# Folding the biases early, q one step ahead, the mask read from SBUF, and narrower scores for the first tile, in a fused attention and mixture-of-experts kernel

## The chip, the cores and the metric

The kernel runs on one core of a Trainium2 chip. The metric is device microseconds of one execution, as the median of several executions; lower is better. The compared kernel before the change took 1164.09 us.

## The reference

Attention over 4 batches, 8 heads, 768 positions and 64 dimensions, and behind it a mixture of 4 experts on the 3072 rows that the attention gives:

```python
scores = (1 / sqrt(64)) * (q @ k.T)                       # per batch and head
rel = pos[:, None] - pos[None, :]
is_global, is_local = pos[None, :] < 8, (rel >= 0) & (rel < 96)
dist = where(is_global & ~is_local, 96, abs(rel))
scores = where(is_global | is_local, scores - slope[h] * dist, -1e9)
x = softmax(scores) @ v                                   # then heads side by side: 3072 x 512
p = domain_probs / (domain_probs.sum(-1) + 1e-9)
out = sum over e of p[:, e] * (relu(x @ w1[e]) @ w2[e])   # w1: 512 x 1024, w2: 1024 x 512
```

A query attends to at most 95 positions before its own and 8 global ones, so a tile of 128 queries needs the keys of its own 128 positions, of the 96 before, and the global ones.

## The kernel before, in words

**Stages.** The program runs in three stretches. First the attention of batch 0 (`attention_early`), alone on the chip, to about 62 us. Then the expert layers of batches 0 and 1, unit by unit, and between their products the attention of batches 1, 3 and 2 (`attention_chain`), which ends within the first 664 us. The rest, to the end, is the expert layers of batches 2 and 3 (`late_batch`); the change does not touch it.

**The expert layers.** They are written with sums of blocks (the scheme of Strassen and Winograd), so that seven products stand for eight. A unit's `first(i)` makes the seven products `pm<-xT,w1s` and `pm<-xB,w1s`, each of six matmuls 384 columns wide; VectorE (DVE) adds such a product to others (`u`, `vv`, `pm`) and, with ScalarE (ACT), leaves `h`. `second(i)` multiplies `h` by w2 (`pm<-w2s,h`, 36 matmuls 512 wide). The weights come by DMA as `raw` and are cast or summed into `w1s` and `w2s` by ACT and GpSimd (POOL). The products have four PSUM buffers of their own.

**The attention of batches 1, 3 and 2.** The work goes by pairs of heads, 12 of them (`order`, lines 626 to 698), and a pair by six tiles t of 128 queries. A tile goes through a pipeline of four stages, one stage at each call of `flow`: `scores` (line 410), `softmax` in two calls (440), `turn_folded` (512), and, when six tiles have gathered, `weigh` (528).

- `prepare_q` and `prepare_k` turn a half of q or k (three tiles) by `pt<-ident,q` or `pt<-ident,k` on TensorE (PE). The value is kept as a rounded part and its remainder, each in the type fp32r: ACT writes the rounded part (`qd<-pt`, `kd<-pt`), DVE the remainder. For q, `spread_q` then copies both parts to the other 64 partitions by DMA from ACT's queue (`qd<-qd`), and the scores wait for that.
- `scores` makes, for each of two heads, two matmuls `ps<-kd,qd`: stationary are 128 columns of q, moving are 256 columns of k's window. So a tile has four. The first tile (t = 0) has no earlier keys, but is 256 wide too.
- `softmax` adds the bias `nbias` (DVE, which also takes the extreme `nmax`), takes the exponential (ACT, `pb`), and one call later scales by the reciprocal of the sum into `pn` (ACT). In `pn` the columns lie folded: global columns share a block with others.
- `turn_folded` transposes `pn` on PE into a PSUM bank `pt`. ACT copies it to SBUF (`pT`), and DVE makes from the same PSUM tile the masked part of the earlier keys with the triangle `newer` (one `scalar_tensor_tensor`).
- `weigh` multiplies `pT` by v (`pt<-pT,v`) and by differences of v (`pt<-pT,vg`), three tiles into one PSUM bank, twice. ACT copies each half to `x`.

The pool `pt` has two PSUM banks. Transposes of q, k and `pn` and the two halves of `weigh` all go through them, and a bank is free again when its last reader is done.

**The order of the work.** A step of the chain (up to a `yield`) is put between the steps of the expert layers by a count: 149 steps before (`count`, line 1425), spread evenly. In the first two stretches and the last one the engines keep the program's order. In the middle one, from about the chain's first step, a scheduler of the language sets the order on each engine from its own estimates, so that an edit in one place can move instructions elsewhere. Instructions of all engines but the DMA issues on SP go through one helper (`emit`, line 42), which is why the profile's lines all name L43.

**The folding.** The table `nbias` (8 heads, 352 columns, bf16) is laid out for the first attention. The other one wants it otherwise, so the chain's first step (line 656) makes the triangle `newer` on POOL, takes a minimum over 96 columns of each head and copies four pieces on DVE.

**A pair's steps, before:** q's first half, k's first half with the spreading of q, q's second half; then t = 0; k's second half, t = 1; the loads of the next pair's q and k, t = 2; the differences of v, t = 3; t = 4; t = 5. These are twelve. v of the pair is loaded at its t = 0.

## Time and profile before

| | |
|---|---|
| three runs | 1163.98, 1164.09, 1166.28 us; median 1164.09 |
| the profiled execution | 1165.77 us, of which 1164.0 us are the span of the profile |
| granted TensorE clock | 0.997 of full speed over the span |
| PE busy | 1137.0 us, 98% |
| DVE, ACT, POOL busy | 882.2, 630.8, 625.8 us (76, 54, 54%) |

Busy time is the time in which an engine had an instruction under way. The order of reading: which engine is busy nearly all of the time, then what its idle time waits for (the releaser, behind the arrow), and what of the other engines' time lies beside it. A group of instructions in a row is named by its tiles, written before the arrow, read behind it, with partitions x elements.

### The profile page before, as it was taken

The numbers are of one execution on the slowest core, as the hardware profiler recorded it, in microseconds if no ns is written. First come the engines' busy times: TensorE is split into PE (matmuls) and PEld (weight loads), VectorE is DVE, ScalarE is ACT, GpSimd is POOL, SyncE is SP. The second block draws the span as 40 slices with busy tenths as digits, with TensorE's granted clock in tenths as the row PEclk, the third lists the DMA queues.
The fourth block names the chain that finished last, engine by engine and source line by source line (L and its number), as shares of the span: only waits on it lengthen the run. The fifth ranks groups of instructions, "written<-read, shape, count | busy, mean of one in ns | idle before, by whom it ended". The sixth has DMA issues, their size and how long they took to land.

```text
span 1164.0 us, 21323 instructions
## 1 busy us (share of the span) xinstructions
PE 1137.0 (98%) x7414; PEld 1056.0 (91%) x7414; DVE 882.2 (76%) x2069; ACT 630.8 (54%) x1777; POOL 625.8 (54%) x606
## 2 busy tenths in 40 slices
PE   7899999999999999999999999999999999999997
PEld 5678898988898989889898899999999999999997
DVE  7978778777878777787777777777777777777776
ACT  6844777877753665665675334444444444444443
POOL 5667656555453234322222427777778855555554
PEclk9999999999999999999999999999999999999999
DMA  9547989787776888987968668888887687676763
GB/s 183 150 141 277 300 216 305 246 258 198 288 245 227 277 264 264 272 245 241 278 187 277 212 217 301 307 301 301 287 314 280 244 296 249 241 258 227 258 228 132
DMA packets 180978, 290.80 MB, mean 250 GB/s; under 512 B 86784, under 2 KB 137472, under 8 KB 168576
## 3 DMA queue, kind: packets, MB, share of 16 engines
q1 hardware_dynamic: 172992, 273.63, 71.6%
q10 hardware_dynamic: 7872, 15.74, 4.7%
q8 instruction: 61, 1.00, 0.4%
q14 instruction: 53, 0.43, 0.1%
HBM read 207.93 MB, written 70.78 MB: 239 GB/s over the span
## 4 chain that ended last, share of the span: by engine, by line
PE 86%; POOL 4%; DVE 4%; DMA 2%; ACT 2%; issue 2%; ACTq 0%; POOLq 0%; DVEq 0%
PE pm L43 36%; PE pf L43 19%; PE X L43 11%; PE Y L43 9%; PE pt L43 7%; PE ps L43 3%; POOL w1s L43 1%; DMA qd<-qd 1%; DVE pb L43 1%; POOL sums L43 1%; PE px L43 1%; POOL xT L43 1%; POOL xB L43 1%; POOL w2s L43 1%; DMA raw<-in_moe_w_dram 1%
## 5 line engine op out<-in xcount | busy, mean ns | idle before, releaser
L43 PE MATMUL pm<-w2s,h 128*128 128x512 f32 x1152 | 284.6, 396 | 2.6 <-DVE h L43 1.6
L43 PEld LDWEIGHTS pm<-w2s,h 128*128 128x128 f32 x1152 | 210.6, 188 | 45.9 <-DVE h L43 3.8
L43 ACT ACTIVATE hf<-pf 128x384 f32<-128x384 f32 x128 | 62.8, 492 | 248.3 <-DVE pf L43 247.1
L43 POOL TENSOR_TENSOR hS<-sf,hS 128x384 fp32r<-128x384 f32 x126 | 134.2, 1084 | 112.4 <-ACT hS L43 111.6
L43 DVE SCALAR_TENSOR_TENSOR acc<-pm,prob,acc 128x512 f32<-128x512 f32 x180 | 132.6, 747 | 34.1 <-PE pm L43 31.7
L43 PE MATMUL pm<-xT,w1s 128*128 128x384 f32 x744 | 148.7, 341 | 0.0
L43 PE MATMUL pf<-xT,w1s 128*128 128x384 f32 x768 | 146.5, 335 | 0.9 <-ACT hf L43 0.7
L43 POOL TENSOR_TENSOR sums<-raw 128x256 f32<-128x256 f32 x54 | 38.8, 737 | 183.3 <-DMA raw<-in_moe_w_dram 91.2
L43 PEld LDWEIGHTS pf<-xT,w1s 128*128 128x128 f32 x768 | 131.4, 188 | 1.7 <-ACT hf L43 1.2
L43 PEld LDWEIGHTS pm<-xT,w1s 128*128 128x128 f32 x744 | 127.7, 188 | 0.8 <-issue 0.7
L43 DVE TENSOR_TENSOR hA<-hf,hA 128x384 fp32r<-128x384 f32 x94 | 84.6, 926 | 50.6 <-ACT hA L43 50.6
L43 PE MATMUL pm<-xB,w1s 128*128 128x384 f32 x574 | 118.4, 345 | 2.5 <-DVE h L43 2.4
L43 ACT ACTIVATE pb<-pb,nmax 128x160 f32<-128x160 f32 (+2 forms) x192 | 84.4, 447 | 48.9 <-DVE nmax L43 44.6
L43 PE MATMUL pf<-xB,w1s 128*128 128x384 f32 x576 | 110.7, 335 | 0.2 <-ACT hf L43 0.2
L43 PEld LDWEIGHTS pm<-xB,w1s 128*128 128x128 f32 x574 | 99.4, 188 | 8.2 <-DVE h L43 2.8
L43 ACT ACTIVATE h<-pm 128x384 fp32r<-128x384 f32 x128 | 62.2, 491 | 70.0 <-DVE pm L43 66.5
L43 PEld LDWEIGHTS pf<-xB,w1s 128*128 128x128 f32 x576 | 98.7, 188 | 0.5 <-ACT hf L43 0.4
L43 POOL TENSOR_TENSOR sf<-hf 128x384 f32<-128x384 f32 x63 | 70.4, 1117 | 43.6 <-ACT hf L43 43.6
L43 ACT COPY pT<-pt 128x256 f32<-128x256 f32 (+2 forms) x216 | 71.1, 329 | 21.7 <-DVE pT L43 12.7
L43 DVE SCALAR_TENSOR_TENSOR h<-pm,h 128x384 fp32r<-128x384 f32 x128 | 69.6, 551 | 10.6 <-ACT h L43 9.1
L43 PE MATMUL Y<-w2b,hS 128*128 128x256 f32 x576 | 74.0, 282 | 0.0
L43 PE MATMUL X<-w2b,hS 128*128 128x256 f32 x576 | 73.9, 282 | 0.0
(168 smaller groups left out, 2250.7 us busy)
## 6 DMA issues: line engine op xcount, KB each, us to landing
w1s<-kept SPq DMA_DIRECT2D x47, 1792.0 KB, 8.0
w2b<-kept SPq DMA_DIRECT2D x224, 256.0 KB, 4.2
kept<-w1s SPq DMA_DIRECT2D x16, 1792.0 KB, 7.7
raw<-in_moe_w_dram SPq DMA_DIRECT2D x43, 512.0 KB, 5.2
kept<-w2s SPq DMA_DIRECT2D x16, 1024.0 KB, 9.2
w2s<-kept SPq DMA_DIRECT2D x16, 1024.0 KB, 6.2
qd<-qd ACTq DMA_DIRECT2D x48, 192.0 KB, 4.3
q<-in_q_dram SPq DMA_DIRECT2D x30, 192.0 KB, 5.1
```

The lines of the kernel that those rows point to most:

```text
L43: ins = fn(*args, **kwargs)
```

## The change

Four edits, all in the attention.

1. **The fold.** It moves into a function `fold_biases`, called at the 27th step of the first attention, before that attention ends. The minimum stays on DVE; the copies, now three, are POOL's. The layout of the first tile's columns changes with it.
2. **q ahead.** The first half of the next pair's q is prepared at the step of t = 4 and spread there. So a pair has 11 steps: k's first half, q's second half; t = 0; k's second half, t = 1; (the load of this pair's v) t = 2; t = 3; the next q's first half, t = 4; t = 5. The loads of the next pair's q and k move to t = 1 and t = 3, the differences of v to t = 4. `count` becomes 138.
3. **The mask.** In `turn_folded` DVE reads ACT's copy `pT` in place of the PSUM tile `pt`.
4. **The first tile.** Its scores are 128 columns wide instead of 256 (four matmuls in each of 12 pairs), and its `pn` is written in four pieces of 96 and 32 columns by ACT, in place of two of 128.

The diff:

```diff
--- before.py
+++ after.py
@@ -410,12 +410,12 @@
     def scores(A, t, got):
 
         both = A.ps.tile([P, 2, 2 * P], F32, name="ps")
-        c0 = (NQT - 1 - t) * PL - (0 if t else NPREV)
+        c0, n = ((NQT - 1 - t) * PL, 2 * P) if t else ((NQT - 1) * PL - NGLOB, P)
         for j in range(2):
-            win = got["k"][:, j].rearrange("p t c -> p (t c)")[:, c0 : c0 + 2 * P]
+            win = got["k"][:, j].rearrange("p t c -> p (t c)")[:, c0 : c0 + n]
             for part in range(2):
                 te.matmul(
-                    both[:, j],
+                    both[:, j, :n],
                     got[("q", t // TPH)][:, j, part, t % TPH * P : (t % TPH + 1) * P],
                     win,
                     start=(part == 0),
@@ -450,8 +450,8 @@
                 new["pcol"] = pcol = slice(P, width) if t == 0 else slice(0, width)
             else:
                 width = PL
-                cols = slice(NPREV, NPREV + P) if t == 0 else slice(0, width)
-                bcol = slice(PL, PL + P) if t == 0 else slice(0, width)
+                cols = slice(0, P) if t == 0 else slice(0, width)
+                bcol = slice(2 * P, 3 * P) if t == 0 else slice(0, width)
                 new["pcol"] = pcol = slice(0, P) if t == 0 else slice(0, width)
                 if t:
                     both = new["both"]
@@ -491,10 +491,16 @@
 
             old["pn"] = pn = A.pb.tile([P, 2 * PL], F32, name="pn")
             if old["t"]:
-                pieces = ((0, pn[:, :PL], pb[:, 0]), (1, pn[:, PL : PL + NGLOB], pb[:, 1, P:]))
+                pieces = (
+                    (0, pn[:, :PL], pb[:, 0]), (1, pn[:, PL : PL + NGLOB], pb[:, 1, P:]),
+                    (1, pn[:, PL + NGLOB :], pb[:, 1, :P]),
+                )
             else:
-                pieces = ((0, pn[:, :P], pb[:, 0, :P]),)
-            for j, dst, src in (*pieces, (1, pn[:, PL + NGLOB :], pb[:, 1, :P])):
+                pieces = [
+                    (j, pn[:, j * (PL + NGLOB) + to : j * (PL + NGLOB) + to + n], pb[:, j, fro : fro + n])
+                    for j in range(2) for to, fro, n in ((0, NGLOB, NPREV), (NPREV, 0, NGLOB))
+                ]
+            for j, dst, src in pieces:
                 ac.activation(dst, src, AF.Copy, scale=zsum[:, j : j + 1])
 
     def turn(A, tile_):
@@ -517,13 +523,14 @@
         for place, at in enumerate((0, PL + NGLOB, P)[: 3 if t else 2]):
             te.transpose(pt[:, place, :], pn[:, at : at + P], ident)
         if t:
-            ve.scalar_tensor_tensor(
-                pT[:NPREV, 0], newer[:NPREV, None, :P].to_broadcast([NPREV, 2, P]), 1.0, pt[:NPREV, :2],
-                op0=ALU.subtract, op1=ALU.mult,
-            )
             for j in range(2):
                 ac.copy(pT[NPREV:, 0, j], pt[j * NGLOB : (j + 1) * NGLOB, 2])
         ac.copy(pT[:, 1], pt[:, :2])
+        if t:
+            ve.scalar_tensor_tensor(
+                pT[:NPREV, 0], newer[:NPREV, None, :P].to_broadcast([NPREV, 2, P]), 1.0, pT[:NPREV, 1],
+                op0=ALU.subtract, op1=ALU.mult,
+            )
 
     def weigh(A, three, x, b):
 
@@ -623,6 +630,16 @@
             flow()
             yield
 
+    def fold_biases():
+
+        po.iota(
+            newer, pattern=[[1, P + NGLOB]], base=1 - NGLOB, channel_multiplier=-1, allow_small_or_imprecise_dtypes=True
+        )
+        po.tensor_scalar(newer, newer, 0.0, 1.0, op0=ALU.is_gt, op1=ALU.mult)
+        ve.tensor_tensor(nbias[:, :, :NPREV], nbias[:, :, :NPREV], nbias[:, :, PL : 2 * P], op=ALU.min)
+        for to, fro in ((PL, NPREV), (NPREV, P), (P, PL)):
+            po.tensor_copy(nbias[:, :, to : to + NGLOB], nbias[:, :, fro : fro + NGLOB])
+
     def attention_chain(bs, A):
 
         tiles, turned = [None] * 4, []
@@ -654,43 +671,42 @@
                     nats[m][n] = next(load(A, {"q": q, "k": k, "v": v}[n], *order[m], n))
 
         fetch_heads(0, "qkv")
-        po.iota(
-            newer, pattern=[[1, P + NGLOB]], base=1 - NGLOB, channel_multiplier=-1, allow_small_or_imprecise_dtypes=True
-        )
-        po.tensor_scalar(newer, newer, 0.0, 1.0, op0=ALU.is_gt, op1=ALU.mult)
-        ve.tensor_tensor(nbias[:, :, :NPREV], nbias[:, :, :NPREV], nbias[:, :, PL : 2 * P], op=ALU.min)
-        for to, fro, n in (
-            (PL, 2 * P + NGLOB, NPREV), (2 * P + NGLOB, NPREV, NGLOB), (NPREV, P, NGLOB), (P, 2 * P + NGLOB, NGLOB),
-        ):
-            ve.tensor_copy(nbias[:, :, to : to + n], nbias[:, :, fro : fro + n])
-        yield
+        yield
+        prepare_q(A, nats[0]["q"], 0, gots[0])
+        flow()
+        yield
+        spread_q(0, gots[0])
         for m, (b, pr) in enumerate(order):
             if pr == PAIRS[0]:
                 xs[b] = None if b == B - 1 else xp.tile([P, NPAIR, S], F32, name="x")
                 if b == B - 1:
                     xd[b] = dp.tile([P, NPAIR, S], F32, name="x_last")
             nat, got = nats[m], gots[m]
-            for part, hf in ((prepare_q, 0), (prepare_k, 0), (prepare_q, 1)):
+            for part, hf in ((prepare_k, 0), (prepare_q, 1)):
                 part(A, nat[part.__name__[-1]], hf, got)
                 flow()
-                if part is prepare_k:
-                    spread_q(0, got)
                 yield
             for t in range(NQT):
-                if t in (1, 2, 3):
-                    if t == 1:
-                        prepare_k(A, nat["k"], 1, got)
-                    elif t == 2:
-                        fetch_heads(m + 1, "qk")
-                    else:
-                        nat["vg"] = differences(A, nat["v"])
+                if t == 1:
+                    prepare_k(A, nat["k"], 1, got)
+                if t == 4 and m + 1 < len(order):
+                    prepare_q(A, nats[m + 1]["q"], 0, gots[m + 1])
+                if t in (1, 2, 4):
                     flow()
+                    if t == 2 and m:
+                        fetch_heads(m, "v")
                     yield
                 flow({"t": t, "pr": pr, "m": m, "v": nat})
                 if t == 0:
                     spread_q(1, got)
-                if t == 0 and m:
-                    fetch_heads(m, "v")
+                elif t == 1:
+                    fetch_heads(m + 1, "q")
+                elif t == 3:
+                    fetch_heads(m + 1, "k")
+                elif t == 4:
+                    if m + 1 < len(order):
+                        spread_q(0, gots[m + 1])
+                    nat["vg"] = differences(A, nat["v"])
                 yield
         while any(tiles):
             flow()
@@ -1047,6 +1063,8 @@
             work_chores()
             if n == 4 * NQT + 1:
                 opening(A)
+            if n == 4 * NQT + 2:
+                fold_biases()
         mix = mixture()
         next(mix)
     Ordered.on = False
@@ -1422,7 +1440,7 @@
 
     SUMUNITS = tuple(per + i for i in (0, 1, 3, 4, 5, 7, 8, 9, 11, 12, 13))
     todo_t = [units[i][1:] for i in range(per)]
-    count, span = 3 * NPAIR * (6 + NQT) + 5, (LATE * 13 * per - 12) * 0.97
+    count, span = 3 * NPAIR * (5 + NQT) + 6, (LATE * 13 * per - 12) * 0.97
     emitted = done = paced = 0
     Ordered.on = True
     for _ in first_sums(1):
```

Where the scheduler moves instructions, three places. The first is PE at the weighing of the second pair of heads (`pT,v` and `pT,vg` are `weigh`'s products, `w2s,h` those of `second`, `w1s` those of `first`). Before:

```order
L43 MATMUL pt<-pT,v 64x128 x4
L43 MATMUL pt<-pT,vg 64x128 x2
L43 MATMUL pt<-pT,v 64x128 x2
L43 MATMUL pt<-pT,vg 64x128 x2
L43 MATMUL pt<-pT,v 64x128 x2
L43 MATMUL pt<-pT,vg 64x128 x2
L43 MATMUL pt<-pT,v 64x128 x2
```

With the change:

```order
L43 MATMUL pt<-ident,k 128x128 x3
L43 MATMUL pt<-pT,v 64x128 x4
L43 MATMUL pt<-pT,vg 64x128 x2
L43 MATMUL pt<-pT,v 64x128 x2
L43 MATMUL pt<-pT,vg 64x128 x2
L43 MATMUL pm<-w2s,h 128x512 x4
L43 MATMUL pt<-pT,v 64x128 x2
L43 MATMUL pt<-pT,vg 64x128 x2
L43 MATMUL pt<-pT,v 64x128 x2
```

Before, the weighing was one run, the two halves in the two `pt` banks. Now four products of `second` stand between the halves, and both halves use one bank. (An F32 product such as `pT,v` shows in the trace as two records.) In 11 of the 12 pairs the halves are apart now, by four or five products.

The second place is ACT around its copy `x<-pt` of the same weighing. Before:

```order
L43 ACTIVATE h<-pm 128x384
L43 DMA qd<-qd 64x768
L43 ACTIVATE h<-pm 128x384
L43 DMA qd<-qd 64x768
L43 ACTIVATE h<-pm 128x384
L43 COPY x<-pt 128x384 x2
L43 ACTIVATE pb,zsum<-pb,nmax 128x128 x2
L43 CAST w1s<-raw_2652 128x512
```

With the change:

```order
L43 ACTIVATE h<-pm 128x384
L43 ACTIVATE pb,zsum<-pb,nmax 128x128
L43 CAST kd<-pt 64x3x128 x2
L43 ACTIVATE zsum<-zsum 128x2
L43 CAST w1s<-raw_2652 128x512
L43 COPY x<-pt 128x384
L43 CAST w1s<-raw_2652 128x256
L43 CAST w1s<-sums 128x512
```

The first copy stood behind nothing of the weights; now it stands behind the casts of k (`kd<-pt`) and a cast of w1 (`w1s<-raw`), which waits for a DMA. Five of the pairs have the cast of w1 there.

The third place is the fold, on DVE. Before, between the sums of `first`'s products:

```order
L43 TENSOR_TENSOR u<-pm,p_1187 128x384
L43 TENSOR_TENSOR nbias<-nbias 128x8x96
L43 TENSOR_TENSOR vv<-pm,u 128x384
L43 COPY nbias<-nbias 128x8x96
L43 COPY nbias<-nbias 128x8x32
L43 TENSOR_TENSOR u<-pm,u 128x384
L43 COPY nbias<-nbias 128x8x32
L43 TENSOR_TENSOR pm<-pm,vv 128x384
L43 COPY nbias<-nbias 128x8x32
L43 TENSOR_TENSOR pm<-pm,p_1187 128x384
```

With the change, between the first attention's last softmax and the first operands of the expert layers:

```order
L43 TENSOR_SCALAR pb,spare<-pb,zsum 128x256 x2
L43 TENSOR_SCALAR zsum,spare<-zsum 128x2
L43 RECIPROCAL zsum<-zsum 128x2
L43 TENSOR_SCALAR pb,spare<-pb,zsum 128x256 x2
L43 TENSOR_TENSOR nbias<-nbias 128x8x96
L43 TENSOR_TENSOR xB_736<-x 128x384
L43 TENSOR_TENSOR xB_735<-xB_736,x 128x384
L43 TENSOR_TENSOR xB_735<-x,xB_735 128x384
```

The minimum alone is left of it on DVE. The copies follow on POOL, behind the last sums of w1 and ahead of the first casts of w2.

## Rows read from the trace of the kernel before

**Rows 1.** The page: busy times, and the chain that ended last by engine.

```profile
PE 1137.0 (98%) x7414; PEld 1056.0 (91%) x7414; DVE 882.2 (76%) x2069; ACT 630.8 (54%) x1777; POOL 625.8 (54%) x606
...
PE 86%; POOL 4%; DVE 4%; DMA 2%; ACT 2%; issue 2%; ACTq 0%; POOLq 0%; DVEq 0%
```

**Rows 2.** Windows: us, busy of PE, PEld, DVE, ACT, POOL (x), PEclk, DMA, GB/s.

```profile
112.00:340.00 228.00, 225.53 (x1392) 203.06 (x1391) 179.75 (x464) 169.32 (x518) 128.27 (x129) 1.00 0.81 250
```

**Rows 3.** Timeline of DVE: start, us, engine, line, operation, tiles, count [idle <-releaser].

```profile
82.97 1.12 DVE L43 TENSOR_TENSOR nbias<-nbias 128x768 bf16<-128x768 bf16 x1
...
84.48 2.21 DVE L43 COPY nbias<-nbias 128x768 bf16<-128x768 bf16 x2
...
87.75 1.29 DVE L43 COPY nbias<-nbias 128x256 bf16<-128x256 bf16 x1
```

**Rows 4.** Timeline of PE around the fold.

```profile
86.39 1.20 PE L43 MATMUL pm<-xB,w1s 128*128 128x384 f32 x6
90.03 1.32 PE L43 MATMUL pm<-xB,w1s 128*128 128x384 f32 x6 [2.43 <-DVE h L43]
```

**Rows 5.** Timeline of DVE and POOL at the end of the first attention.

```profile
62.28 0.56 DVE L43 TENSOR_TENSOR xB<-x 128x384 f32<-128x384 f32 x1 [4.78 <-ACT x L43]
...
67.08 1.86 POOL L43 TENSOR_TENSOR xT<-xB,xT 128x768 fp32r<-128x768 f32 x1 [11.05 <-ACT xT L43]
```

**Rows 6.** Timeline of PE, the scores that waited longest for q's spreading.

```profile
523.46 0.50 PE L43 MATMUL ps<-kd,qd 128*128 128x256 f32 x2 [1.19 <-DMA qd<-qd]
```

**Rows 7.** Timeline of PE, the weighings that waited for a bank.

```profile
273.78 0.66 PE L43 MATMUL pt<-pT,v 128*64 128x128 f32 x8 [0.37 <-PE ps L43]
...
315.39 0.66 PE L43 MATMUL pt<-pT,v 128*64 128x128 f32 x8 [0.82 <-ACT pT L43]
```

**Rows 8.** Groups by form on PE: tiles, shapes, count | busy us, mean ns | idle.

```profile
L43 PE MATMUL ps<-kd,qd 128*128 128x256 f32 x288 | 46.7, 282 | 1.6 <-DMA qd<-qd 1.6
...
L43 PE MATMUL pt<-ident,pn 128*128 128x128 f32 x204 | 35.8, 273 | 1.3 <-ACT pn L43 1.3
```

**Rows 9.** Timeline of PE: F32 matmuls, then others of 512, 384, 128, 256 columns.

```profile
62.30 2.85 PE L43 MATMUL pm<-x,w1s 128*128 128x384 f32 x8 [0.58 <-ACT x L43]
64.99 0.81 PE L43 MATMUL pm<-xB,w1s 128*128 128x384 f32 x2
...
118.76 3.80 PE L43 MATMUL pm<-w2s,h 128*128 128x512 f32 x16
...
520.77 0.33 PE L43 MATMUL pm<-xT,w1s 128*128 128x384 f32 x1
520.95 0.38 PE L43 MATMUL pt<-ident,pn 128*128 128x128 f32 x2
...
521.86 0.40 PE L43 MATMUL ps<-kd,qd 128*128 128x256 f32 x2
```

**Rows 10.** Timeline of PE at the end of the second pair's weighing.

```profile
195.21 0.39 PE L43 MATMUL pt<-pT,v 128*64 128x128 f32 x4
195.43 0.39 PE L43 MATMUL pt<-pT,vg 128*64 128x128 f32 x4
195.75 0.44 PE L43 MATMUL pm<-xT,w1s 128*128 128x384 f32 x1
```

**Rows 11.** Groups by form on ACT, from 112 to 340 us.

```profile
L43 ACT CAST kd<-pt 64x384 fp32r<-64x384 f32 x22 | 10.4, 473 | 0.8 <-PE pt L43 0.7
...
L43 ACT CAST w1s<-raw 128x512 fp32r<-128x512 f32 x11 | 6.8, 617 | 3.7 <-DMA raw<-in_moe_w_dram 2.4 <-PE pm L43 1.3
...
L43 ACT ACTIVATE zsum<-zsum 128x2 f32<-128x2 f32 x33 | 6.6, 201 | 0.5
...
L43 ACT COPY x<-pt 128x384 f32<-128x384 f32 x8 | 3.7, 481 | 2.4 <-PE pt L43 2.4
```

**Rows 12.** Timelines of ACT and PE at the first pair's first tile.

```profile
120.58 0.62 ACT L43 CAST w1s<-raw 128x512 fp32r<-128x512 f32 x1 [1.94 <-DMA raw<-in_moe_w_dram]
...
123.83 0.62 PE L43 MATMUL pt<-ident,pn 128*128 128x128 f32 x2 [1.26 <-ACT pn L43]
```

## The prediction

> **What bounds the kernel now.** I read the busy times first, then the chain that ended last, then PE's own idle time. PE is busy for 98% of the span, and 86% of the chain lies on it [rows 1]. The attention chain's stretch says the same from closer by: of 228 us PE is busy for 225.5, while DVE has 48 us free, ACT 59 and POOL 100, at the full clock (1.00, the 2.4 GHz level) [rows 2]. So time on the other three costs nothing until PE waits for its result, and the change can win in two ways only: take a wait from PE, or take PE work away. A price is given below for PE alone unless a waiter is named.
>
> **The fold.** Of DVE's five instructions on `nbias`, which stand between the sums of `first`, the four long ones take 1.12 + 2.21 + 1.29 = 4.62 us [rows 3]. PE waits right behind for DVE's `h`, 2.43 us, and its next six matmuls take 1.32 us where six just before took 1.20 [rows 4]. I put all of it down to the fold: -2.43 - 0.12 = **-2.55**. Bounds: 0, if another sum is as late, and -4.6, all that DVE is given. I take the idle time because it was PE's, and half of DVE's time was hidden already. In the new place the minimum (1.12) falls into an idle stretch of DVE of 4.78 us, which ends on ACT, and the three copies into 11.05 us in which POOL waits for ACT [rows 5]. Three copies as slow as the slowest of DVE's, 1.29, are 3.9 us, so the cost is nothing; without this cover, DVE's 1.12 would delay the first `xB`.
>
> **q one step ahead.** Two scores waited for the spreading DMA: 1.19 us the one [rows 6], and 1.6 us the whole group, all of it on `qd<-qd` [rows 8]. The spreading now comes two steps of the chain before its readers, some 8 us by 149 steps over the 600 us between 62 and 664. **-1.65**; bounds 0 and that. The second half of q is spread at t = 0 as before and read at t = 3. The loads of q, k and v move too, each to four steps ahead of its first reader on SP's queue, where q and k had six: 16 us by the same step, and nothing I price. If one is late, PE's transposes of k at the next pair's start are the first to wait.
>
> **The mask from SBUF.** A `pt` bank was held until DVE had read it. Two weighings began late for a bank or its `pT`: 0.37 and 0.82 us [rows 7]. Now ACT's copy frees the bank. **-1.19**; bounds 0 and that. In exchange DVE's mask waits for ACT's three copies, and what is queued behind it on DVE, the sums that PE waits for, waits too. A step or more, 4 us, lies between a tile's mask and its weighing, so I price that wait at nothing and keep it as a rival.
>
> **Narrower scores.** 48 matmuls go from 256 to 128 columns. Two of 256 take 0.40 us, one 0.28, so one every 0.12 us [rows 8, 9]; sixteen of 512 take 3.80 [rows 9], one every 0.23. The line through both gives 0.066 us for 128 columns and -2.6 us in all. But every one of these matmuls has weights of its own, and the nearest row of that kind is the transposes of `pn`: two of 128 columns take 0.38, one 0.27, so one every 0.11 [rows 8, 9]. The first matmul behind the short ones of a weighing also shows 0.44 us [rows 10] where another of its shape shows 0.33 [rows 9]: 0.11 of weights not hidden. I take 0.11, 48 x (0.11 - 0.12) = **-0.5**. At the other end stand F32 matmuls: eight records of 384 columns, two to a matmul, start within 2.69 us [rows 9], 0.22 us for 128 columns, and 48 x 0.10 = +5.0.
>
> On this the Trainium skill speaks with two voices on one page, "TensorE: Matmul & The Clock Gate". Its section "Back-to-back issue gap" has 134 cycles for 128 columns and 262 for 256, which would be 53 ns and 2.6 us in all; its section "LDWEIGHTS (loading the stationary operand)" has 1/1.2 ns for a column, 107 ns for 128, which would leave about half a microsecond of gain, and with that the rows agree.
>
> **What the scheduler moves: the weighing.** Twelve runs of short products become 23: the halves stand apart in 11 of 12 pairs, with four or five products of w2 between (the order on PE). A run's end costs 0.32 - 0.22 = 0.10 from its last group to the next kind of matmul, and 0.11 in that matmul [rows 9, 10]: 11 x 0.21 = **+2.3**. Bounds: 0, if the w2 products hide it, and 11 x 0.34 = 3.8 with an entry like the exit.
>
> **A new wait for the bank.** Both halves now use one bank, so the second waits for ACT's copy of the first, 0.48 us, behind two casts of k, 0.47 each, and one of 0.20 for `zsum`: 1.6 us, or 2.2 with the 0.62 of a w1 cast, as in five pairs [rows 11]. PE's cover is ten short products at 0.11 (two start within 0.22 [rows 10]) and four or five at 0.23 [rows 9], 2.0 to 2.2 us. So seven pairs wait for nothing and five for 0.2 at most by these, with four products between: **+1.0**. Bounds: 0 and +5, when the cast's DMA is late too: the eleven casts of that form waited 2.4 us for it here [rows 11].
>
> **The first tile's `pn`.** PE waited 1.26 us for it once, behind an ACT that waited 1.94 for a w1 load [rows 12]. Now second exponential and `pn` stand behind both casts of `sums` on ACT, but PE comes to it six w2 products (1.4 us) later: **+0.2**, bounds -1.3 and +2.7, two more casts at 0.62 and PE's own 1.4. The 24 more pieces of `pn`, none wider than a cast of k at 0.47 [rows 11], are under 12 us over 600 on ACT, which has 59 free in every 228.
>
> **Sum.** -2.55 - 1.65 - 1.19 - 0.5 + 2.3 + 1.0 + 0.2 = -2.4 us. The profiled execution took 1165.77 (span 1164.0), so its like would be 1163.4; that execution stands 1.7 above the median of the runs shown, 1164.09. Against that median the forecast is **1161.7**. A measurement of this kernel tells 0.2% from no change, 2.3 us: faster is below 1161.8, slower above 1166.4.
>
> **The rivals.**
>
> *Narrow fp32r at the F32 pace.* If 128 columns lose the type's speed, the +5.0 stands in place of -0.5: 1161.7 + 5.5 = **1167.2**, slower. It decides as soon as a narrow score starts every 0.2 us. For it: no row shows an fp32r matmul under 256 columns, and the F32 rows show that PE has such a pace. Against it: at a column a cycle, 2.4 GHz, the rows of 512 and 256 columns would take 0.213 and 0.107, and each is some 0.01 over; nothing grows as they narrow. Chance 0.14.
>
> *The weighing waits for a weight load.* ACT's copy between the halves stands behind the w1 cast in five pairs, and if the load is as late as at 120.58 us, 1.94 [rows 12], PE waits 5 x 1.9 = 9.5 at most: 1161.7 - 1.0 + 4 to 9.5 is 1165 to 1170, **1168** for the middle, slower. It decides from some 1 us a pair. Against it: the eleven casts lost 2.4 us together, not each. Chance 0.10.
>
> *The width halves.* If the weights are hidden, as the line of widths has it, the scores give -2.6: **1159.6**, faster. The cycle table of the Trainium skill named above would give the same. Against it: the `pn` transposes at 0.11. Chance 0.12.
>
> *The costs don't show.* Split and bank wait hide beside 512-wide products and only the gains are left: 1161.7 - 3.5 = **1158.2**, faster. Chance 0.15.
>
> *A wait in place of the ones removed.* DVE's mask holds the sums of `first` while ACT is behind with its pieces and casts; 72 tiles, 60 of them with a mask, need only lose 0.04 us each to give back the 2.4. **1164**, no change. For it: PE's waits for `h` and for `pn` are on just these two engines [rows 4, 12]. Chance 0.19.
>
> My own sum keeps 0.30, 0.17 of it below 1161.8 and 0.13 above. So faster 0.17 + 0.12 + 0.15 = 0.44, same 0.13 + 0.19 = 0.32, slower 0.24. The range from 1156.0 (the gains alone with the width halved, -8.0) to 1168.5 (either slower rival at its middle) leaves out the far ends of the second and fourth rival, under 0.2. The likeliest case alone has 1159 to 1164.5.
>
> **What would show it.** DVE without `nbias` near 85 us, and PE without 2.4 us behind it; no idle time of `ps<-kd,qd` on `qd<-qd`. For the scores: 48 matmuls of 128 columns, one every 0.11 us by my value, 0.07 or 0.22 by the rivals'. Twenty-three runs of weighing, and PE's idle time before a run's second half below 1.5 us over all pairs; if it stands there with ACT as the releaser and more than 4 us, the second rival is right. New idle time of `pm<-w2s,h` behind DVE's `h`, where DVE had waited for ACT's `pT`, would be the last one. I am wrong altogether if the late batches, from 664 us on, change their length.

## The result, and the profile after

The change made the kernel slower: 1175.82 us median against 1165.07 for the kernel before on the same chip, ratio 1.0095 with a 95% interval of 1.0079 to 1.0111. The forecast was 1161.7, in a range that ended at 1168.5.

The profiled execution took 1175.91 us, with a span of 1174.1. The page's busy times and its chain by engine:

```profile
PE 1139.7 (97%) x7414; PEld 1052.7 (90%) x7414; DVE 893.0 (76%) x2065; ACT 634.7 (54%) x1801; POOL 627.2 (53%) x609
...
PE 78%; DVE 7%; ACT 6%; POOL 3%; issue 3%; DMA 1%; SPq 1%; ACTq 0%; DVEq 0%; POOLq 0%
```

The span grew by 10.1 us, PE's busy time by 2.7 and so its idle time by 7.4. The chain says behind whom PE stands: PE has 78% of it instead of 86, DVE and ACT have 13% instead of 6 [rows 1]. But the loss is not idle time alone. From unit 2 to unit 31 of the table below PE's busy time grew by 6.1 us (559.5 to 565.6) and its idle time by 7.2 (5.9 to 13.1). The whole span hides this, since ahead of the first unit PE was busy 3.2 us less in the trace after, where the granted clock differs: the trace of before has 3.4 us at 0.50, from 54.83 us, and that of after has no such stretch.

PE's groups by form (busy us, mean ns | idle us before them, by releaser) show where the idle time went:

```profile
L43 PE MATMUL ps<-kd,qd 128*128 128x256 f32 x240 | 38.5, 282 | 0.0
...
L43 PE MATMUL pt<-ident,pn 128*128 128x128 f32 x204 | 36.6, 276 | 6.1 <-ACT pn L43 4.9 <-DVE kd L43 0.7
...
L43 PE MATMUL pt<-pT,v 128*64 128x128 f32 x288 | 27.1, 281 | 5.0 <-ACT x L43 2.9 <-ACT piece L43 1.8 <-DVE kd L43 0.2
...
L43 PE MATMUL ps<-kd,qd 128*128 128x128 f32 x48 | 6.7, 263 | 0.0
```

The waits that were to go are gone: no score waits for q's DMA [rows 8], and the two waits of weighings, 1.2 us together [rows 7], have gone too. In their place the weighings wait 5.0 us, for ACT's copies `x` and `piece` (the batch kept in DRAM), and the transposes of `pn` wait 6.1 instead of 1.3 [rows 8].

When it was lost can be read from PE's timeline: 32 units of `second(i)` follow each other, and the start of a unit's first `pm<-w2s,h` is taken as a mark. Times since unit 0's mark, worked out from those starts, in us (the last four columns are experiments, told below):

| unit | before | after | mask from PSUM | mask waits, PSUM | short POOL pieces | fold alone |
|---|---|---|---|---|---|---|
| 2 | 44.8 | 42.9 | 42.9 | 42.9 | 42.9 | 42.1 |
| 13 | 265.7 | 270.3 | 269.7 | 271.5 | 271.1 | 262.7 |
| 20 | 396.5 | 402.1 | 400.6 | 402.6 | 403.9 | 393.7 |
| 27 | 540.6 | 552.2 | 543.9 | 546.3 | 550.0 | 537.2 |
| 31 | 610.2 | 621.6 | 613.1 | 615.5 | 619.0 | 606.9 |

Against before, the change gains 1.9 us up to unit 2 (the fold; 2.7 with the fold alone), loses 6.5 from 2 to 13, 1.0 to 20, 6.0 from 20 to 27, and nothing after it. The late batches last 499 us in both. From the first mark on, the granted clock is 1.00 up to unit 31 in all six traces, except in that with the short pieces (below).

**The loss from unit 2 to 13** is not the mask's: with the mask from PSUM 5.9 of the 6.5 us are still there. By the marks of the experiments some 3.6 come with q one step ahead (220.6 us for the stretch with the fold alone, 224.2 with both) and some 2.6 with the narrow scores (226.8 with these too). What they consist of is told with those experiments and in the part on the prediction.

**The loss from unit 20 to 27** stands in a chain of four engines, once in each of four pairs of heads. At its head is the mask. DVE's sixty mask instructions, before and after (minimum/median/maximum ns):

```profile
L43 DVE SCALAR_TENSOR_TENSOR pT<-newer,pt x60: 398/407/419, 131.1 to 642.5; 96x256 f32<-96x256 bf16 x60
```

```profile
L43 DVE SCALAR_TENSOR_TENSOR pT<-newer,pT x60: 409/422/2617, 131.7 to 652.1; 96x256 f32<-96x256 bf16 x60
```

Most take 0.42 us as they did 0.41, but some up to 2.6. The longest, on DVE, and what POOL did at the time:

```profile
486.52 2.62 DVE L43 SCALAR_TENSOR_TENSOR pT<-newer,pT 96x256 f32<-96x256 bf16 x1
489.06 0.54 DVE L43 TENSOR_TENSOR u<-pm,u 128x384 f32<-128x384 f32 x1
489.53 0.55 DVE L43 TENSOR_TENSOR pm<-pm,vv 128x384 f32<-128x384 f32 x1
489.99 0.55 DVE L43 TENSOR_TENSOR pm<-pm,p 128x384 f32<-128x384 f32 x1
```

```profile
486.47 2.38 POOL L43 TENSOR_TENSOR sums<-sums,raw 128x1024 fp32r<-128x1024 f32 x1
```

DVE's mask began 0.05 us after POOL's instruction and ended 0.29 behind its end (486.52 + 2.62 = 489.14, 486.47 + 2.38 = 488.85). The sums of `first` stand behind the mask on DVE, ACT's `h` behind the sums, the casts of k behind `h`, and the copy of the weighing's first half behind those:

```profile
490.11 0.49 ACT L43 ACTIVATE h<-pm 128x384 fp32r<-128x384 f32 x1 [2.62 <-DVE pm L43]
490.50 0.46 ACT L43 CAST kd<-pt 64x384 fp32r<-64x384 f32 x1
490.86 0.49 ACT L43 ACTIVATE h<-pm 128x384 fp32r<-128x384 f32 x1
491.37 0.47 ACT L43 CAST kd<-pt 64x384 fp32r<-64x384 f32 x1
491.87 0.48 ACT L43 COPY piece<-pt 128x384 f32<-128x384 f32 x1
```

And PE, whose second half needs that copy's bank:

```profile
488.24 0.66 PE L43 MATMUL pt<-pT,v 128*64 128x128 f32 x8
...
489.48 1.14 PE L43 MATMUL pm<-xB,w1s 128*128 128x384 f32 x5
492.40 0.44 PE L43 MATMUL pt<-pT,v 128*64 128x128 f32 x4 [1.78 <-ACT piece L43]
```

The same `sums<-sums,raw` holds the mask at 529.25, 571.07 and 613.00 us too, each time for 1.81 us in all, and PE then waits 0.97, 0.95 and 0.94. These four waits are 4.6 of the 5.9 us that PE stands idle from unit 20 to 27; the rest is before `pn`. With the mask from PSUM PE has no idle time in this stretch.

That is no accident of four places. Of the mask instructions that took over 0.5 us, every one ended 0.27 to 0.29 us after the end of the POOL instruction that was running when it started: thirteen in this trace, and nineteen in that of the experiment with the old order of steps. The difference to the kernel before is one operand. There DVE read `newer` from SBUF and `pt` from PSUM; now both are in SBUF. (The edit also makes the mask wait for ACT's copy; an experiment takes the two apart.)

### The profile page after: what moved, and what is told of

Same layout as the page of the kernel before. It is cut to its first block, busy times and chain, and to the rows that moved or that the text cites. A ratio compares the mean times of both kernels' runs of the same rounds, so it can differ in the third digit from the quotient of the medians.

```text
span 1174.1 us, 21404 instructions
## 1 busy us (share of the span) xinstructions
PE 1139.7 (97%) x7414; PEld 1052.7 (90%) x7414; DVE 893.0 (76%) x2065; ACT 634.7 (54%) x1801; POOL 627.2 (53%) x609
## 4 chain that ended last, share of the span: by engine, by line
PE 78%; DVE 7%; ACT 6%; POOL 3%; issue 3%; DMA 1%; SPq 1%; ACTq 0%; DVEq 0%; POOLq 0%
PE pm L43 32%; PE pf L43 19%; PE X L43 11%; PE Y L43 9%; PE pt L43 5%; PE ps L43 2%; DVE pb L43 2%; POOL w1s L43 1%; ACT pb L43 1%; DVE qd L43 1%; ACT pT L43 1%; SPq L43 1%; ACT pn L43 1%; ACT h L43 1%; DVE u L43 1%
## 5 line engine op out<-in xcount | busy, mean ns | idle before, releaser
L43 ACT ACTIVATE pn<-pb,zsum 128x32 f32<-128x32 f32 (+3 forms) x228 | 70.8, 367 | 17.3 <-DVE zsum L43 16.6
```

What stands on the lines that cost most here:

```text
L43: ins = fn(*args, **kwargs)
```

## The experiments

All twelve were timed in five rounds against the kernel before on the same chip; ratios are to it. Two theories went in. The first: with both operands in SBUF DVE waits for POOL's running instruction, and what is queued behind it is late. The second: the new order of the steps (the split weighing, q's remainder on DVE) makes the loss alone.

**One part undone at a time.** The mask from PSUM again:

```diff
         if t:
+            ve.scalar_tensor_tensor(
+                pT[:NPREV, 0], newer[:NPREV, None, :P].to_broadcast([NPREV, 2, P]), 1.0, pt[:NPREV, :2],
+                op0=ALU.subtract, op1=ALU.mult,
+            )
             for j in range(2):
                 ac.copy(pT[NPREV:, 0, j], pt[j * NGLOB : (j + 1) * NGLOB, 2])
         ac.copy(pT[:, 1], pt[:, :2])
-        if t:
-            ve.scalar_tensor_tensor(
-                pT[:NPREV, 0], newer[:NPREV, None, :P].to_broadcast([NPREV, 2, P]), 1.0, pT[:NPREV, 1],
-                op0=ALU.subtract, op1=ALU.mult,
-            )
```

> The change with one part undone: DVE reads the mask from PSUM again. First theory (the mask): with two operands in SBUF the mask instruction waits for GpSimd's long sums, 0.9 to 2.6 us instead of 0.42 at seven places after 445 us, and the sums of first, h and the x copy behind it are late; then this gives 1168 to 1171 us, no mask instruction takes over 0.5 us, and the second halves of the weighings at 490 to 617 us wait under 0.3 us instead of 1.1 to 1.9. Rival (the order of the steps): the split of the weighing and the place of q's remainder on DVE make the time alone; then this stays at 1174 to 1176.

Measured: 1168.64 us, 1.0027 (1.0016 to 1.0037). Its mask instructions and PE's two groups:

```profile
L43 DVE SCALAR_TENSOR_TENSOR pT<-newer,pt x60: 401/407/418, 129.6 to 641.7; 96x256 f32<-96x256 bf16 x60
...
L43 PE MATMUL pt<-ident,pn 128*128 128x128 f32 x204 | 37.0, 276 | 5.3 <-ACT pn L43 4.2 <-DVE kd L43 0.3 <-ACT w1s L43 0.3
...
L43 PE MATMUL pt<-pT,v 128*64 128x128 f32 x288 | 27.1, 281 | 0.0
```

No mask takes over 0.42 us, and the weighing's idle time of 5.0 is 0. So the bank that both halves share was not the price: with DVE on time, ACT's copy comes on time. The `pn` wait stays, 5.3 us: that belongs to something else.

The old order of the steps, with the mask still from SBUF (`attention_chain`'s loop and `count` as before, fold and scores as changed):

> The change with one part undone: the old steps of a pair, q prepared in its own pair (149 steps). First theory (the mask): the long mask instructions stay, PE waits for what is behind them, and this gains 2 to 5 us only, for the split weighing that goes: 1171 to 1174. Rival (the order of the steps): the weighing is one run again and no pn waits for a reciprocal behind q's remainder; 1163 to 1167.

Measured: 1174.63 us, 1.0076 (1.0064 to 1.0089), just over what the first theory gave, and far from the second's 1163 to 1167. PE waits at other places, and nineteen masks take over 0.5 us, the longest 1.45:

```profile
L43 PE MATMUL pt<-pT,v 128*64 128x128 f32 x288 | 29.1, 298 | 4.5 <-ACT pT L43 3.9 <-DVE qd L43 0.6
...
L43 PE MATMUL ps<-kd,qd 128*128 128x128 f32 x48 | 7.9, 274 | 5.3 <-DMA qd<-qd 5.3
```

Not all of this loss is PE's waiting. Around its two longest waits, 3.78 us for `qd` at 153 us and 2.23 for `pT` at 240.6, the granted clock fell to 0.50 (the 1.2 GHz level), for 6.8 us from 152.24 and 3.4 from 240.99.

Both undone, so that the early fold and the narrow scores alone are left:

> The change with both undone: early fold and 128 columns alone are left. Both theories: 1161 to 1163 (the fold's 2.5 us and 0.5 of the scores below 1164.1). If the scores or their pn pieces cost something of their own, over 1165.

Measured: 1165.54, 0.9999 (0.9989 to 1.0009). The kernel before took 1165.74 on this chip, so the gain of 1 to 3 us is not there, and the scores, their pieces or their order cost what the fold gained. The fold alone (below) gave 0.9987, with an interval that overlaps this one.

The wide scores again, with two pieces of `pn`:

> The change with one part undone: the first tile's scores are 256 wide again, pn in two pieces, the fold has four copies on GpSimd. By the 48 matmuls at 0.109 us instead of 0.118 in the trace this is the same within 1 us: 1175 to 1177. If the four pieces of pn on ACT hold the x copy or pn back, it is below 1174.

Measured: 1172.35, 1.0060 (1.0047 to 1.0073). Below 1174: narrowing cost 3.5 thousandths here, though the matmuls became faster (below). Most of it goes through the mask: of 5.2 us by the marks 3.9 lie from unit 20 to 27, where the four masks behind `sums<-sums,raw` take 1.29 to 1.34 us with wide scores and 1.81 to 2.62 after.

**What of the mask it is: the operand or the wait for ACT.** One kernel keeps the wait and gives the operand back to PSUM, by a one-column copy that DVE's write has to follow:

```diff
         ac.copy(pT[:, 1], pt[:, :2])
         if t:
+            ac.copy(pT[:NPREV, 0, 0, :1], pt[:NPREV, 0, :1])
             ve.scalar_tensor_tensor(
-                pT[:NPREV, 0], newer[:NPREV, None, :P].to_broadcast([NPREV, 2, P]), 1.0, pT[:NPREV, 1],
+                pT[:NPREV, 0], newer[:NPREV, None, :P].to_broadcast([NPREV, 2, P]), 1.0, pt[:NPREV, :2],
                 op0=ALU.subtract, op1=ALU.mult,
             )
```

> The change, but the mask reads PSUM again and still waits for ACT's copies (a one-column copy into its destination, 60 more of some 0.2 us on ACT). First theory (one SBUF operand more, so DVE waits for GpSimd's running instruction): the mask instructions are all near 0.41 us and the time is that without the SBUF mask, 1167 to 1170. Rival (waiting for ACT is what costs): 1174 to 1178.

Measured: 1171.7, 1.0058 (1.0042 to 1.0074), between the two. Its masks:

```profile
L43 DVE SCALAR_TENSOR_TENSOR pT<-newer,pt x60: 405/417/419, 131.0 to 645.2; 96x256 f32<-96x256 bf16 x60
```

None is held any more. From unit 20 to 27 this kernel takes 143.7 us, with the mask from PSUM 143.3, after 150.1: there the operand is nearly all of it. What it loses against the mask from PSUM, it loses earlier, 2.0 us of 2.4 before unit 20, with 60 more copies on ACT; whether by the copies or by the wait was not separated. Over whole runs the split is less one-sided than in these traces: the operand is 1.0095 - 1.0058 = 3.7 thousandths, 4.3 us, and the wait with its copies 1.0058 - 1.0027 = 3.1, each give or take some 2. (The traced execution of this kernel was 2.5 us faster than its median.)

The other kernel keeps the operand and shortens what POOL runs:

```diff
-        po.tensor_copy(high.bitcast(F32R), low)
-        po.tensor_tensor(low.bitcast(F32R), low, high, op=ALU.subtract)
+        for n in range(4):
+            po.tensor_copy(high.bitcast(F32R)[:, n], low[:, n])
+        for n in range(4):
+            po.tensor_tensor(low.bitcast(F32R)[:, n], low[:, n], high[:, n], op=ALU.subtract)
```

> The change, with GpSimd's 1024-element split of the w2 sums cut into pieces of 256. First theory: no mask instruction is held for over 1 us any more, the second halves of the weighings at 490 to 617 us wait some 1 us less each, 4 to 5 us together: 1170 to 1173. Rival (waiting for ACT): no difference, 1175 to 1177.

Measured: 1173.66, 1.0077 (1.0063 to 1.0091), a little over what was expected and below the rival's. The mask that had taken 1.81 us at 571.07, on DVE, and the pieces on POOL:

```profile
570.04 1.00 DVE L43 SCALAR_TENSOR_TENSOR pT<-newer,pT 96x256 f32<-96x256 bf16 x1
```

```profile
569.34 3.00 POOL L43 TENSOR_TENSOR sums<-sums,raw 128x256 fp32r<-128x256 f32 x4
```

It is 1.00 now: DVE gets in behind a piece and does not wait for the last. From unit 20 to 27 it takes 146.1 us, 4.0 less than after, as expected there; over the whole it keeps 2.6 by the marks, since from unit 2 to 20 it loses 1.8. Its trace shows two causes there: behind PE's wait of 2.08 us for `pn`, at 122.38, the granted clock was 0.50 for 3.4 us (after, that wait was 1.84 us and the clock stayed at 1.00), and PE waited 0.78 us for a load of k.

The mask alone, put into the kernel before:

> The kernel before with the mask from SBUF alone. First theory (a second SBUF operand makes DVE wait for GpSimd, and the wait for ACT comes on top): 1170 to 1175, some mask instructions over 1 us, each ending some 0.28 us behind the end of a GpSimd instruction. By the prediction's term it would be 1.2 us faster than before, 1163 to 1164.

Measured: 1176.66, 1.0096 (1.0079 to 1.0113). This one part costs as much as the whole change. Nineteen masks take over 0.5 us, and in the old order the loss falls on other places than after:

```profile
L43 PE MATMUL ps<-kd,qd 128*128 128x256 f32 x288 | 47.0, 283 | 4.8 <-DMA qd<-qd 4.2 <-DVE kd L43 0.6
...
L43 PE MATMUL pt<-ident,pn 128*128 128x128 f32 x204 | 35.7, 275 | 2.2 <-ACT pn L43 2.2
...
L43 PE MATMUL pt<-pT,v 128*64 128x128 f32 x288 | 27.4, 284 | 3.2 <-ACT pT L43 2.5 <-DVE qd L43 0.6
```

The trace has two stretches of 3.4 us at a granted clock of 0.50 besides, from 87.15 and 155.42 us, at waits of PE's of 2.43 and 3.60; how much of the 9.6 thousandths is theirs was not separated.

**The fold, q ahead and the width apart.** The fold alone, moved as in the change (its four copies on POOL):

> The kernel before with the fold alone moved (its four copies on GpSimd). By the prediction's term -2.55 us against before, 1161.5 on the old median and 1163.2 on the last one. Rival: PE meets the next late sum and nothing is gained, within 1 us of before.

Measured: 1163.11, 0.9987 (0.9978 to 0.9996), faster than before and the fastest of all that were run. PE where it had waited 2.43 us [rows 4], now without idle time:

```profile
86.94 3.28 PE L43 MATMUL pm<-xT,w1s 128*128 128x384 f32 x18
90.06 2.24 PE L43 MATMUL pm<-xB,w1s 128*128 128x384 f32 x12
```

The fold and q one step ahead, with wide scores and the mask from PSUM:

> Early fold and q one step ahead alone: the mask from PSUM, scores of 256 columns, pn of the first tile in two pieces. Against the fold alone (0.9987 of before) the prediction's terms give -1.65 for the DMA wait, +2.3 for the split weighing and +1.0 for the bank: 1.6 us more, 0.999 to 1.001 of before. Rival (the pn that waits for the reciprocal behind q's remainder on DVE): 3 us more or above, 1.0015 to 1.003.

Measured: 1166.1, 1.0006 (0.9994 to 1.0018), inside what the prediction's own terms gave against the fold alone. The groups say that the gains came and what ate them:

```profile
L43 PE MATMUL ps<-kd,qd 128*128 128x256 f32 x288 | 46.0, 282 | 0.0
...
L43 PE MATMUL pt<-ident,pn 128*128 128x128 f32 x204 | 36.6, 275 | 3.6 <-ACT pn L43 2.9 <-DVE kd L43 0.3
...
L43 PE MATMUL pt<-pT,v 128*64 128x128 f32 x288 | 27.1, 281 | 0.0
```

The DMA wait (1.6 before, 1.3 with the fold alone) and the weighings' wait (1.2) are gone. The `pn` transposes wait 3.6 instead of 1.2, and 1.1 of this is at the first pair's first tile (2.34 instead of 1.23). So PE's idle time as a whole is no longer than with the fold alone. Its busy time is 3.8 us longer, by the two pages, the fold alone first:

```profile
PE 1132.6 (98%) x7414; PEld 1053.4 (91%) x7414; DVE 880.9 (76%) x2065; ACT 631.0 (54%) x1777; POOL 627.4 (54%) x610
```

```profile
PE 1136.4 (98%) x7414; PEld 1052.0 (91%) x7414; DVE 880.5 (76%) x2065; ACT 628.0 (54%) x1777; POOL 629.7 (54%) x610
```

The eleven splits of the weighing are 3.5 us of that: from the start of the last product of one half to that of the first of the other each takes 0.30 to 0.37 us more than the same matmuls at their plain spacing (0.11 for a product of the weighing, 0.23 for one of w2, 0.17 for one of `first`).

The fold and 128 columns in the plain order, which leaves `pn` in two pieces:

```diff
-        c0 = (NQT - 1 - t) * PL - (0 if t else NPREV)
+        c0, n = (NQT - 1 - t) * PL, 2 * P if t else P
```

> The kernel before with the early fold and first-tile scores of 128 columns in their plain order, so that pn keeps its two pieces. Against the same with four pieces (1165.5): if the narrow matmuls themselves cost, the same, 1165 to 1166; if the pieces of pn or the order cost what the narrow scores seemed to, 1162 to 1163.5.

Measured: 1164.59, 0.9994 (0.9985 to 1.0003), between the two: slower than the fold alone by 0.7 thousandths, with overlapping intervals.

The same at 240 columns, where PE's work is nearly that of 256:

> Early fold, and first-tile scores of 240 columns instead of 256, which gives the scheduler other costs but PE nearly the same matmuls. If the narrow scores lost their 1.5 us by the order that the scheduler makes of them, this is as slow as the 128 columns (0.9994 of before); if by the matmuls themselves, it is as fast as the fold alone (0.9987).

Measured: 1172.77, 1.0062 (1.0047 to 1.0077). Sixteen columns fewer cost 7.5 thousandths, more than 128 fewer. It can't be the matmuls, which start every 0.111 us instead of 0.118 (medians). What is left is above all the order. One place of it, on ACT and then PE, at the first pair's first tile:

```profile
118.54 0.62 ACT L43 CAST w1s<-raw 128x512 fp32r<-128x512 f32 x1 [2.30 <-DMA raw<-in_moe_w_dram]
...
120.80 0.62 ACT L43 CAST w1s<-sums 128x512 fp32r<-128x512 f32 x1 [1.24 <-POOL sums L43]
122.70 0.62 ACT L43 CAST w1s<-sums 128x512 fp32r<-128x512 f32 x1 [1.28 <-POOL sums L43]
123.22 0.69 ACT L43 ACTIVATE pn<-pb,zsum 128x128 f32<-128x128 f32 x2
```

```profile
123.68 0.62 PE L43 MATMUL pt<-ident,pn 128*128 128x128 f32 x2 [3.63 <-ACT pn L43]
124.06 2.78 PE L43 MATMUL pm<-w2s,h 128*128 128x512 f32 x6
```

In the kernel before `pn` stood ahead of the second cast of `sums`, and PE waited 1.26 us [rows 12]; now it stands behind it, POOL's sum for that cast is 1.28 us late, and PE waits 3.63. This one exchange on ACT is 2.4 us. And the granted clock fell right behind the wait; the window shows 0.50 as PEclk (us, busy of PE, PEld, DVE, ACT, POOL, PEclk, DMA, GB/s):

```profile
124.20:127.61 3.41, 3.41 (x11) 2.83 (x11) 1.55 (x3) 2.80 (x11) 1.66 (x3) 0.50 0.86 353
```

The six products of w2 start every 0.43 us there instead of 0.23, 1.2 us more. The rest of the loss, such as 2.2 us more before `h` from unit 13 to 20 than with the fold alone, was not followed up.

Last, a try for a better version: the fold, and q's first half spread in the step that prepares it, in the old order of steps:

> A try for a better version: early fold, and q's first half spread in the step that prepares it, one step before it was, in the old order of steps. If the DMA wait of the scores goes (1.6 us in the kernel before) and nothing else moves, 0.997 to 0.998 of before; if ACT's queue stands behind DVE's remainder, 0.999 or more.

Measured: 1169.59, 1.0033 (1.0020 to 1.0046), worse than without. The scores no longer wait for the DMA but 1.6 us for DVE's `kd`; the first `pn` waits 2.27 us, and `h` costs PE 3.8 us instead of 1.8 with the fold alone. At two of these waits, at 123 and 416 us, the granted clock was 0.50 for 3.4 us each.

## Why the prediction was wrong

**The mask: the step that failed.** The text gave it -1.19 with bounds of 0 and that, and priced what is queued behind it on DVE at nothing. It looked at when the mask starts, not at how long it runs. Put on top of the other three parts it costs 1.0095 - 1.0027 = 6.8 thousandths, 7.9 us, where a gain of 1.2 was forecast; on the kernel before alone, 9.6 thousandths. In the traces 6.4 us of it, from unit 20 to 27, are DVE held by POOL (150.1 against 143.7 with the same waits and a PSUM operand). Over whole runs the operand alone is shown for 3.7 of the 6.8 thousandths; the other 3.1 went with the wait for ACT and the 60 copies, and stay open between the two.

The forecast gain had no row for it either: of the two waits in rows 7 one names ACT's `pT` and one PE's own scores, none DVE, and both are gone with q ahead alone, where the mask still reads PSUM.

The last rival had the place, DVE's mask holding the sums of `first`, but put it on ACT and at 2.4 us. By the sign that the prediction gave, the second rival would have been read as right, since PE waits 4.6 us before second halves with ACT as the releaser. But ACT stood behind DVE's mask there and not behind a load of w1 (the rows at 490 us), and with the mask from PSUM the wait is 0.

It could have been read beforehand. The text summed DVE's long instructions on `nbias` [rows 3] and did not ask why they are long. A copy of 128x256 is among them at 1.29 us; another of the same form, not shown there, and its neighbour on DVE, in the kernel before:

```profile
87.08 0.28 DVE L43 COPY nbias<-nbias 128x256 bf16<-128x256 bf16 x1
87.28 0.55 DVE L43 TENSOR_TENSOR pm<-pm,vv 128x384 f32<-128x384 f32 x1
```

And POOL at the time:

```profile
86.95 0.77 POOL L43 TENSOR_SCALAR newer<-newer 128x160 bf16<-128x160 bf16 x1
87.69 2.49 POOL L43 TENSOR_TENSOR w2s<-raw,w2s 128x512 fp32r<-128x512 f32 x2
```

The same copy of 128x256 takes 0.28 us at 87.08 and 1.29 at 87.75 [rows 3], where it started 0.06 us after POOL's first `w2s<-raw,w2s`, and ended 0.08 behind its end, while the sum from PSUM ran its 0.55 beside POOL. So here a copy of DVE's within SBUF, like the minimum with its two operands there (1.12 us beside POOL's sums of w1, 0.55 without), was not as long as its form says while POOL ran a sum of two tensors. Beside POOL's `newer<-newer` the copy was not held; what sets that instruction apart was not tested.

The Trainium skill has the rule that spoke against this part, in its page "SBUF — State Buffer", section "SBUF: two separate sides": a DVE instruction with two SBUF inputs and a GpSimd instruction that reads SBUF need the same pair of ports, whichever starts first has it for its whole length, and the other is blocked. The traces agree: 2.62 us instead of 0.42, and 0.41 with a PSUM operand in the same place.

**The fold: right.** -2.55 was forecast; the marks show 2.7 up to unit 2 (44.8 to 42.1 with the fold alone), and the whole kernel gains 1.7 us (1163.11 against 1164.83). DVE's minimum in its new place, after the change:

```profile
57.48 0.55 DVE L43 TENSOR_TENSOR nbias<-nbias 128x768 bf16<-128x768 bf16 x1
60.79 0.95 DVE L43 TENSOR_TENSOR xB<-x 128x384 f32<-128x384 f32 x1 [2.75 <-ACT x L43]
```

It takes 0.55 us, half of what it took beside POOL [rows 3], inside DVE's idle time; and PE has no idle time where it had 2.43:

```profile
87.39 3.28 PE L43 MATMUL pm<-xT,w1s 128*128 128x384 f32 x18
90.51 2.24 PE L43 MATMUL pm<-xB,w1s 128*128 128x384 f32 x12
```

**q one step ahead: the gain right, the total about right, two prices wrong.** The DMA wait went (-1.65, with no idle time left on `qd<-qd`). The split weighing cost 3.5 us where +2.3 was said, inside its bound of 3.8. PE at such a split, in the trace after:

```profile
280.43 0.39 PE L43 MATMUL pt<-pT,vg 128*64 128x128 f32 x4
280.75 1.19 PE L43 MATMUL pm<-w2s,h 128*128 128x512 f32 x4
281.87 0.44 PE L43 MATMUL pt<-pT,v 128*64 128x128 f32 x4
```

From the last four records of one half to the other half this takes 281.87 - 280.43 = 1.44 us, where two products at 0.11 and four at 0.23 would take 1.14. Of the 0.30 too much, the text had the end of a run (0.10 and 0.11) but only in its bound the start of the next. (In six of the eleven pairs products of `first` stand between the halves, and not of w2 as the text had it.)

The new wait for the bank, +1.0, is 0 once the mask is right. What the text did not have is `pn`: 2.3 us more of idle time (3.6 against 1.2 with the fold alone), most of it on ACT's `pn`. Of this, 1.1 is the first tile's (below), and 1.2 the other waits'. At 274 us, in the trace after, `pn` was late because DVE's reciprocal stood behind two remainders of the next q and the mask. Whether this holds for the others was not tested. These waits and the waits that went, 2.5 us against the fold alone, about cancel, so that what is left as the loss with q ahead, 1.9 thousandths or 2.2 us, is PE's busy time, the split above all. That the total came out near its forecast of 1.65 is in part luck: a split and a `pn` that cost more, and a bank wait that cost nothing, offset each other.

**The narrow scores: the size right, the sign of the whole wrong.** The forecast of 0.11 us for 128 columns holds:

```profile
273.94 0.56 PE L43 MATMUL ps<-kd,qd 128*128 128x128 f32 x4
275.19 0.33 PE L43 MATMUL pt<-ident,pn 128*128 128x128 f32 x1 [0.69 <-ACT pn L43]
```

Four take 0.56 us, one 0.26 (its group's mean is 263 ns), so one every 0.10; the median over 36 of them is 0.109. Neither the F32 pace (0.22) nor the halved width (0.066) shows. But 48 x 0.01 us was never what the edit is worth: with four pieces it costs 2.1 thousandths on top of fold and q ahead (1.0006 to 1.0027, from unit 2 to 31 of the traces 1.7 us of idle time and 1.3 of busy) and 3.5 in the whole change, where longer masks are most of it. The 240 columns show that a change of the order, with the waits and the clock that came with it, can do that and more; how much of the 2.1 is order and how much the pieces on ACT was not separated.

**The first tile's `pn`:** +0.2 was said, with up to +2.7; the wait there grew by 0.6 on PE's first transpose after the change, by 1.1 with fold and q ahead alone, by 1.5 with the mask from PSUM, and by 2.4 in the kernel of 240 columns, all inside that bound.

The parts add up as they were put in one after the other: fold -1.3 thousandths, q ahead +1.9, narrow scores with four pieces +2.1, mask from SBUF +6.8, together +9.5. The first is good to 0.9, and each of the others, a difference of two ratios, to some 1.5 to 2, so that the 1.9 and the 2.1 are little more than their noise, and the 6.8 is far above it. They are no constants of the edits, since each was measured in one order; the mask costs 6.8, 7.7 (old order, 0.9999 to 1.0076) and 9.6 thousandths in the three that were tried.

## What to carry to other kernels

Before an operand moves from PSUM to SBUF to free a bank sooner, look at what the instruction's other operand is and what POOL runs at the time: two copies of one form that differ fourfold in length in the trace are the sign. Then ask what is queued behind it on DVE; the price here was not the 10 us by which the masks' busy time grew (24.6 to 34.6), but above all the four places where PE needed what came next.

Where a scheduler orders the engines from its own estimates, an edit's own time and the order that comes with it are two things. A control that changes the estimate and next to nothing else, such as the 240 columns, tells how large the second can be before the first is credited or blamed. And where two traces are compared, compare the granted clock of the stretch too: here it fell behind long waits of PE's, in some traces and not in others.

## What the runs showed of the hardware that was not expected

In the traces after and with the old order of steps, DVE's mask, held behind POOL's running instruction, ended 0.27 to 0.29 us after its end, whichever instruction of POOL's it was: two-tensor ones of 256, 512 and 1024 elements, and a cast of 1024. So a start inside POOL's last 0.14 us costs nothing (0.42 us in all), and an earlier one costs the rest of POOL's remainder. It goes the other way too: with POOL's sums in pieces of 256, one that started in the last third of a microsecond of a held mask took 0.90 to 0.92 us instead of 0.73. And a waiting mask is not always next: with the short pieces, five masks that started in the last 0.1 us of a POOL instruction ended behind the next one.

In six traces of the experiments the granted clock was 0.50 (the 1.2 GHz level) for 3.4 us, once 6.8, in the stretch of the units, each time at or just behind a wait of PE's of 2.1 to 3.8 us; in other traces waits of up to 2.74 us left it at 1.00.
